# A gated mix of two attentions: path A's denominators inverted an iteration later, fetched by ScalarE, late products moved to the iteration's end

## The chip, the cores and the metric

The kernel runs on one core of a Trainium2 chip. The metric is the time of the whole launch on the device, in microseconds (us); before the change it is 987.2 us (median of three runs, 984.97 to 989.04).

## What is computed

```python
g = _sigmoid((x * gate_w).sum(-1, keepdims=True))
# path A, linear attention with a learned feature map, 16 heads of 28
phi_q = concat([softmax(pq), softmax(-pq)]); phi_k = the same of pk
kv  = einsum("bhsf,bhsd->bhfd", phi_k, v)
num = einsum("bhqf,bhfd->bhqd", phi_q, kv)
den = einsum("bhqf,bhf->bhq", phi_q, z) + 1e-6
a = (num / den) @ wo_A
# path B, softmax attention, 16 heads of 28
b = softmax(q k^T / sqrt(28)) v @ wo_B
out = g * a + (1 - g) * b          # 2048 tokens, 448 columns, float32
```

## The kernel before, in words

The order of the instructions on TensorE, VectorE, ScalarE and GpSimd is the order in which the code is written; only SyncE's transfers are ordered by a scheduler. Every transfer, on whatever queue, also takes the next of eight completion counters in turn, and waits until the transfer that had this counter before it has landed.

The change lies in one loop (L703), where path A's queries are handled and path B's values begin. Its iterations are counted here by q, from 0 to 26; y is q - 1. The 2048 queries are taken in eight blocks of 256, numbered 0 to 7. For one block b these steps follow each other:

- In iteration y = 2b + 4, `numer` (L522) forms the numerators of block b on TensorE in two PSUM banks `pn`. `normalize1` (L377) copies them with ScalarE into the SBUF tile `oUa` (L381); one row in 32 of it holds a denominator. Two small transfers spread these rows over 128 partitions, tile `dena` (L384). Before the change SyncE issues them.
- `normalize2` (L387): VectorE inverts `dena` (L389). Two transfers write the inverses to DRAM, `rda` (L393), and one transfer of 512 KB reads them back with each row repeated for 32 partitions, `rsa` (L394). Before the change it is called at y = 2b + 5, an odd iteration, behind the feature work.
- `normalize3` (L398): VectorE multiplies `oUa` by `rsa` (L400), at y = 2b + 8, in the middle of the iteration.
- `normalize4` (L403): ScalarE rounds the product to `oTa` (L408), and GpSimd forms what the rounding left (L409), at y = 2b + 9.
- `out_a` (L536) projects block b with `woA_s` on TensorE, 12 matmuls into `poa` for each 128 queries, at y = 2b + 10 and 2b + 11; ScalarE scales the result to `ga` (L544), which goes to DRAM (`gad`, L545).

Between these stand, in the same iterations: the projection of the queries `pq` (L109, 11 matmuls, to q = 15) with its features (`pcq`, `extq`, `featq`), the transposes of the features `pft` (L516) that ScalarE copies to `fT` (L519), the values of path B `pvb` (11 matmuls of L109, copied to `vb` by L691, from q = 18), and `mx_unit` (L238): four matmuls `pmd` and `pmb` (L260), two ScalarE operations `rl` (L264) and two VectorE operations on `pmb` and `rl` (L265, written "ISA" in the lists of order). From q = 19 to q = 25 an iteration holds two such units, one in its middle and one at its end.

PSUM is given out in turn: `pn`, `poa`, `pft`, `pq` and `pvb` share four banks in a ring, and the four banks of one `mx_unit` are used again by the next. So TensorE's next transposes wait for the ScalarE copy that empties the bank four places earlier in the ring.

Of the kernel before, what the change touches and what calls it, by code (L numbers as in the profile page):

```python
# [17 lines left out]
P = 128  # L18
# [3 lines left out]
DH = 28  # L22
GW = 112
NG = 4
NT = S // P
# [16 lines left out]
def gated_mix_kernel(ctx, tc, xT, wqkB, wvB, wvA, wkAT, wqAT, phi, woA, woB,  # L42
# [7 lines left out]
    nc = tc.nc  # L50
# [18 lines left out]
    def ps_mx(nm):  # L69
        return ps.tile([P, 512], F32, tag="mx", name=nm, bufs=psn[1])  # L70
# [94 lines left out]
    def take_acts():  # L165
        while acts:
            acts.pop(0)()
# [20 lines left out]
    def mx_query(gq):  # L188
        g, qb = divmod(gq, NQ)
        mxs[("qc", gq)] = mx_rows(mx_tile("qc", f"qc{gq}", 3), range(4), q_d[g], range(4), qb * 512)  # L190
# [19 lines left out]
    def pair_query(gq, hp):  # L210
        g, qb = divmod(gq, NQ)
        mxs[("qp", gq, hp)] = mx_rows(mx_tile("qc", f"qp{gq}_{hp}", 3), range(4), q_d[g],
                                      (2 * hp, 2 * hp + 1) * 2, qb * 512)

    def mx_fin():
        while mxs["fin"]:
            mxs["fin"].pop(0)()
# [20 lines left out]
    def mx_unit():  # L238

        u = mxs["u"]  # L240
        if u == NF:
            return
        mx_fin()
        mxs["u"] = u + 1
        gq, r = divmod(u, 16)
        g, qb = divmod(gq, NQ)
        c, qt = divmod(r, 4)
        hp, b = divmod(c, 2)
        col = 64 * gq + 16 * b + 4 * qt + 2 * hp
        if r in (4, 9) and gq + 1 < GM:  # L250
            pair_query(gq + 1, r // 9)
        if r == 4 and gq + 1 == GM:
            mx_query(GM)
        qc, kc = mxs[("qp", gq, hp)], mxs[("kp", g, c)]

        pm = [ps_mx(f"pm{'ddbb'[j]}{u}_{j % 2}") for j in range(4)]
        for j in range(4):
            i = (j + 2) % 4
            js = slice(32 * i, 32 * i + DH)
            nc.tensor.matmul(pm[j], qc[js, qt * P:(qt + 1) * P], kc[js, :], start=True, stop=True,  # L260
                             tile_position=(32 * i, 0))
        for i in range(2):
            rl = rlp.tile([P, 512], F32, tag="rl", name=f"rl{u}_{i}", bufs=psn[2])
            nc.scalar.activation(rl, pm[i], AF.Relu)  # L264
            nc.vector.tensor_tensor_reduce(rl, pm[2 + i], rl, 1.0, LOWEST, ALU.add, ALU.max,  # L265
                                           part[:, col + i:col + i + 1])
        if gq + 1 < GM and qt == 3 and qb == NQ - 1:
            pair_load(g + 1, c)
        if gq + 1 == GM and qt == 3:
            mx_load(GM // NQ, c)  # L270
        if r == 15:
            mx_reduce(gq)
# [104 lines left out]
    def normalize1(pool, pn, nm, n):  # L377

        oU = pool.tile([P, n, 512], F32, tag="oU", name=f"oU{nm}", bufs=2 * n - 1)
        for i in range(n):  # L380
            (nc.scalar.copy if n == 2 else nc.vector.tensor_copy)(oU[:, i, :], pn[i])  # L381
        den = pool.tile([P, n, 16], F32, tag="den", name=f"den{nm}", bufs=2)
        for i in range(n):
            nc.sync.dma_start(den[:, i, :], oU[DH:P:32, i, :])  # L384
        return oU, den

    def normalize2(pool, oU, den, nm, n):  # L387

        nc.vector.reciprocal(den, den)  # L389
        rd = dr.tile([4, n * 512], F32, tag=f"rd{n}", name=f"rd{nm}", bufs=2)  # L390
        rs = pool.tile([P, n, 512], F32, tag="rs", name=f"rs{nm}", bufs=n)
        for k in range(n):
            nc.sync.dma_start(rd[:, k * 512:(k + 1) * 512], den[:, k, :])  # L393
        nc.sync.dma_start(rs.rearrange("p n q -> p (n q)"),  # L394
                          rd.unsqueeze(1).to_broadcast([4, 32, n * 512]))
        return oU, rs

    def normalize3(oU, rs, n):  # L398

        (nc.gpsimd if n == 1 else nc.vector).tensor_mul(oU, oU, rs)  # L400
        return oU
# [58 lines left out]
    fk, va, fq, fT_of, num, oTs = {}, {}, {}, {}, {}, {}  # L460
# [242 lines left out]
    for i in range(2 * NT + 11):  # L703
        t, q = i, i - NT
        y = q - 1
        tb = y // 2
        take_acts()
        if t < NT and t % 2 == 0:
            mx_unit()
            passes = (55 if t < NT - 4 else 44) + (4 if t >= 4 else 0)  # L710
            pace["n"], pace["at"] = 4 if t >= 4 else 0, [k * passes // 4 for k in range(1, 4)]
        if q in (0, 1):
            take_exps()

        if t % 2 == 0 and 0 <= t - 4 < NT:
            kv_add(t - 4)
            kv_add(t - 3)
        if q == 2:
            bk_s.close()
            ta_s = ExitStack()  # L720
            ta = ta_s.enter_context(tc.tile_pool(name="ta", bufs=1, reuse_waits="tile"))
            stg = ta_s.enter_context(tc.tile_pool(name="stg", bufs=2, reuse_waits="tile"))
            KV = ta.tile([P, 2, P], F32, name="KV")
            kvT = kv_copy()
            ps_s_.close()
            ps = ps_s_.enter_context(tc.tile_pool(name="psq", bufs=1, space=PSUM, reuse_waits="tile"))
            psn[0] = 4
            woA_s = weights(3, "woA_s")
            wvB_s = weights(2, "wvB_s")
            take_exps()  # L730
        if t < NT:
            pk = ps_s(f"pk{t}")
            tok_major(pk, t, wkA_s, D, tick)
            fk[t] = features1(pk, f"k{t}", nc.gpsimd)
            take_exps(1)
        if 0 <= q < NT:
            pq = ps_s(f"pq{q}")
            tok_major(pq, q, wqA_s, D)
        if q == 0:
            fk[NT - 1] = features2(fk[NT - 1], f"k{NT - 1}")  # L740
        if q in (1, 2):
            fq[q - 1] = features2(fq[q - 1], f"q{q - 1}")
        if 0 <= q < NT:
            fq[q] = features1(pq, f"q{q}", nc.vector if q in (4, 6) else nc.gpsimd)
        if 0 <= t - 1 < NT - 1:
            fk[t - 1] = features2(fk[t - 1], f"k{t - 1}")
        if q in (0, 1) or q >= 8:
            mx_unit()
        if y >= 9 and y % 2 and tb - 4 < 8:
            oTs[tb - 4] = normalize4(ta, num.pop(tb - 4), f"a{tb - 4}", 2)  # L750
        if q > 0:
            take_exps(int(q < NT))
        if q == 3:
            kv_out(kvT)
        if 2 <= q - 1 < NT:
            fq[q - 1] = features2(fq[q - 1], f"q{q - 1}")
        take_subs()
        if t == 1:
            pair_load(0, 3)
        if y >= 8 and y % 2 == 0 and tb - 4 < 8:  # L760
            num[tb - 4] = normalize3(*num[tb - 4], 2)
        if y >= 5 and y % 2 and tb - 2 < 8:
            num[tb - 2] = normalize2(ta, *num[tb - 2], f"a{tb - 2}", 2)
        if t < NT:
            value_a(t)
            if t % 2 and t < NT - 4:
                proj_qk(NP + t // 2, ev)
        if q in (0, 1):
            proj_qk(NP + 6 + q, ev)
        take_lows()  # L770
        if 2 <= i < 6:
            fold(wqA_s, "q", i - 2)
        if q == 1:
            ev_s.close()
        if q == 2:
            part_loads("woA", woA, D, "woA")
            raws["wvB"] = [f32(ta.tile([P, 2, 512], F32R, tag="oT", name=f"wvB_raw{b}", bufs=4))[:, :, :D]
                           for b in (0, 2)]
            for i in range(2):
                nc.sync.dma_start(raws["wvB"][i], wvB[:, 2 * i:2 * i + 2, :])  # L780
        if q in (4, 6):
            split_part(woA_s, "woA", D, (q - 4) // 2, nc.gpsimd)
        if q in (8, 10):
            split_part(wvB_s, "wvB", D, (q - 8) // 2)
        if q == 1:
            gates()
        if y >= 4 and y % 2 == 0 and tb - 2 < 8:
            numer(tb - 2)
        if y < 9 or y % 2:
            if y >= 2 and y - 2 < NT:  # L790
                turn(y - 2)
        if 0 <= y - 10 < NT:
            out_a(y - 10)
            out_a2(y - 10)
        if y >= 9 and y % 2 == 0 and y - 2 < NT:
            turn(y - 2)
        if NT + 3 <= q < NT + 10:
            mx_unit()
        if q == NT + 6:
            ps_s_.close()  # L800
            ps = ps_s_.enter_context(tc.tile_pool(name="psv", bufs=1, space=PSUM, reuse_waits="tile"))
            psn[:2] = 2, 6
        if q == NT + 2:
            bd_s.close()
            vb = [value_tile(0)]
        if 0 <= q - NT - 2 < 8:
            value_b(q - NT - 2)
# [434 lines left out]
```

## Time and profile before

| what | value |
|---|---|
| time of the profiled execution | 986.38 us |
| span in its trace | 984.6 us |
| TensorE busy | 973.6 us, 99% |
| VectorE, ScalarE, GpSimd busy | 716.0, 752.2, 228.1 us |
| mean granted TensorE clock | 0.998 |
| moved by DMA | 84.49 MB, all on SyncE's queue but 1.44 MB of instructions |

The trace lists each instruction with its start, length, and what ended the idle time of its engine just before it. PE is TensorE, PEld its weight load, DVE VectorE, ACT ScalarE, POOL GpSimd, SPq the queue of SyncE. A matmul's length is modelled and overlaps the next; the distance between starts is the measure. The stage that the change touches lies between 204 and 332 us of the span.

### The profile page before, as it was taken

What the parts mean: (1) busy time and instruction counts of PE and PEld (TensorE: products, weight loads), DVE (VectorE), ACT (ScalarE), POOL (GpSimd) and SP (SyncE); (2) the same over time, 40 slices, a digit from 0 to 9 for tenths busy, and PEclk for the clock granted to TensorE, in tenths of its full rate; (3) what the DMA queues carried; (4) which work ended last, traced back from release to release, by engine and by line L of the source; (5) the groups of instructions that cost most, each with busy time, mean ns of one, the idle gap of its engine ahead of it and who ended that gap; (6) DMA issues with size and microseconds to landing.
All of it is one profiled execution on the core that took longest, in us unless ns stands there. A gap on an engine that the chain in (4) does not pass through costs nothing.

```text
span 984.6 us, 22550 instructions
## 1 busy us (share of the span) xinstructions
PE 973.6 (99%) x8510; PEld 602.9 (61%) x8510; DVE 716.0 (73%) x1338; ACT 752.2 (76%) x1442; POOL 228.1 (23%) x236
## 2 busy tenths in 40 slices
PE   9999999999999999999999999999999999999998
PEld 8777877787767765555555555545555555555555
DVE  5566767888735678888888888888888888885112
ACT  4455655577855688988988888888898898887662
POOL 1135435586732810031011011011011011010010
PEclk9999999999999999999999999999999999999999
DMA  8873110112223234121132121122231222100441
GB/s 295 315 255 114 37 53 32 44 51 73 96 91 100 85 120 130 38 62 41 62 93 69 39 63 41 60 82 66 69 83 41 64 63 65 41 21 30 142 150 57
DMA packets 56140, 84.49 MB, mean 86 GB/s; under 512 B 17216, under 2 KB 23984, under 8 KB 56032
## 3 DMA queue, kind: packets, MB, share of 16 engines
q1 hardware_dynamic: 56032, 83.06, 27.2%
q8 instruction: 67, 1.10, 0.5%
q14 instruction: 41, 0.34, 0.1%
HBM read 54.86 MB, written 27.78 MB: 84 GB/s over the span
## 4 chain that ended last, share of the span: by engine, by line
PE 89%; DMA 6%; DVE 2%; ACT 1%; issue 1%; SPq 0%; DVEq 0%; ACTq 0%
PE g L861 29%; PE pv L1006 26%; PE pk L127 4%; PE pva L127 4%; PE pqk L109 3%; PE g L288 3%; PE pq L109 3%; PE poa L109 3%; PE pob L109 3%; PE pmd L260 3%; DMA dena<-oUa 2%; PE pvb L127 2%; DMA qkd<-ev 2%; PE pvb L109 1%; DMA xraw<-in_xT_dram 1%
## 5 line engine op out<-in xcount | busy, mean ns | idle before, releaser
L869 ACT ACTIVATE p<-g 128x512 f32<-128x512 f32 x1020 | 525.6, 609 | 83.0 <-PE g L861 82.2
L295 DVE TENSOR_REDUCE part<-g 128x1 f32<-128x512 f32 x704 | 442.5, 684 | 83.9 <-PE g L288 82.4
L861 PEld LDWEIGHTS g<-qst,kst 32*128 32x128 f32 x3060 | 221.3, 183 | 215.2 <-DVE part L295 195.0
L861 PE MATMUL g<-qst,kst 32*128 32x512 f32 x3060 | 338.3, 420 | 0.1
L1006 PE MATMUL pv<-p,vb 128*32 128x512 f32 x2048 | 273.0, 605 | 0.0
L288 PE MATMUL g<-kc,qc 28*128 28x512 f32 x704 | 233.5, 495 | 0.0
L265 DVE CUSTOM_DVE_ANT_0 rl<-pmb,rl 128x512 f32<-128x512 f32 x160 | 103.2, 682 | 45.0 <-ACT rl L264 44.9
L400 POOL TENSOR_TENSOR oUb<-oUb,rsb 128x512 f32<-128x512 f32 x15 | 19.3, 1286 | 488.9 <-DMA rsb<-rdb 419.7
L264 ACT ACTIVATE rl<-pmd 128x512 f32<-128x512 f32 x160 | 87.6, 602 | 33.5 <-PE pmb L260 30.1
L288 PEld LDWEIGHTS g<-kc,qc 28*128 28x128 f32 x704 | 86.5, 182 | 0.3
L1006 PEld LDWEIGHTS pv<-p,vb 128*32 128x32 f32 x2048 | 40.6, 108 | 66.1 <-issue 64.2
L109 PE MATMUL pqk<-XH,wB 128*128 128x512 f32 x192 | 59.5, 398 | 0.8 <-DVE ev L569 0.8
L260 PE MATMUL pmb<-kp,qp 28*128 28x512 f32 x160 | 43.1, 498 | 3.3 <-DVE part L265 2.7
L109 PE MATMUL poa<-woA_s,oTa 128*128 128x448 f32 x192 | 45.1, 384 | 0.0
L568 ACT CAST ev<-pqk 128x512 fp32r<-128x512 f32 x28 | 16.0, 588 | 38.0 <-PE pqk L109 21.5
L1017 DVE SCALAR_TENSOR_TENSOR acc<-pob,gate,acc 128x448 f32<-128x448 f32 x12 | 8.2, 684 | 48.4 <-PE pob L109 48.4
L109 PEld LDWEIGHTS pqk<-XH,wB 128*128 128x128 f32 x192 | 35.3, 188 | 9.9 <-issue 1.5
L569 DVE TENSOR_TENSOR ev<-pqk,ev 128x512 fp32r<-128x512 f32 x28 | 18.9, 689 | 29.5 <-ACT ev L568 29.4
L260 PE MATMUL pmd<-kp,qp 28*128 28x512 f32 x160 | 40.1, 497 | 0.0
L109 PEld LDWEIGHTS poa<-woA_s,oTa 128*128 128x128 f32 x192 | 35.7, 193 | 7.0 <-issue 2.5
L127 PE MATMUL pk<-wkA_s,XH 128*128 128x448 f32 x128 | 39.4, 382 | 0.0
L109 PE MATMUL pq<-wqA_s,XH 128*128 128x448 f32 x128 | 37.4, 375 | 1.3 <-ACT oUa L381 1.3
(158 smaller groups left out, 1054.5 us busy)
## 6 DMA issues: line engine op xcount, KB each, us to landing
qkd<-ev SPq DMA_DIRECT2D x28, 512.0 KB
qst<-qkd SPq DMA_DIRECT2D x64, 112.0 KB
kst<-qkd SPq DMA_DIRECT2D x64, 112.0 KB
od<-oTb SPq DMA_DIRECT2D x48, 112.0 KB
rsa<-rda SPq DMA_DIRECT2D x8, 512.0 KB
oL<-od SPq DMA_DIRECT2D x8, 512.0 KB
rsb<-rdb SPq DMA_DIRECT2D x15, 256.0 KB
gad<-ga SPq DMA_DIRECT2D x16, 224.0 KB
```

The lines of the kernel that those rows point to most:

```text
L109: nc.tensor.matmul(dst, l, r, start=i == 0, stop=i == len(todo) - 1)
L127: nc.tensor.matmul(dst[:, :n], l, r, start=i == 0, stop=i == len(todo) - 1, skip_group_check=True)
L260: nc.tensor.matmul(pm[j], qc[js, qt * P:(qt + 1) * P], kc[js, :], start=True, stop=True, tile_position=(32 * i, 0))
L264: nc.scalar.activation(rl, pm[i], AF.Relu)
L265: nc.vector.tensor_tensor_reduce(rl, pm[2 + i], rl, 1.0, LOWEST, ALU.add, ALU.max, part[:, col + i:col + i + 1])
L288: nc.tensor.matmul(pm, mxs[("qc", gq)][js, qt * P:(qt + 1) * P], mxs[("kc", gq // NQ, kb)][js, :], start=True, stop=True, tile_position=(3 ...
L295: nc.vector.tensor_reduce(part[:, col:col + 1], pm, AX.X, ALU.max)
L400: (nc.gpsimd if n == 1 else nc.vector).tensor_mul(oU, oU, rs)
L569: nc.vector.tensor_sub(e[:, 1, :], pq, f32(e[:, 0, :]))
L861: nc.tensor.matmul(st[j], kst_of[(gq // NQ, kt // 4)][js, k, (kt % 4) * P:(kt % 4 + 1) * P], qst_of[gq][js, q, :], start=n == 0, stop=n == ...
L869: nc.scalar.activation(p, st[j], AF.Exp, scale=SCALE)
L1006: nc.tensor.matmul(pv[32 * j:32 * j + 32, :], vb[kt // 8][:, kt % 8, 4 * g + j, :], pt[j], start=kt == 0, stop=kt == NT - 1, tile_position ...
```

## The change

Three things are done, for path A alone (n = 2 in the code; path B calls the same functions with n = 1 and stays).

- The two transfers of a block's denominators are issued by ScalarE, behind its copies of the numerators, and no longer by SyncE.
- The inversion with its three transfers is done at y = 2b + 6, an even iteration, right behind the `mx_unit` in its middle, and no longer at y = 2b + 5.
- The products of blocks 4 to 7 (y = 16, 18, 20, 22) stand at the end of their iteration, behind its second `mx_unit` where there is one. Those of blocks 0 to 3 stay.

```diff
         for i in range(n):
-            nc.sync.dma_start(den[:, i, :], oU[DH:P:32, i, :])
+            (nc.scalar if n == 2 else nc.sync).dma_start(den[:, i, :], oU[DH:P:32, i, :])
         return oU, den
...
         if q in (0, 1) or q >= 8:
             mx_unit()
+        if y >= 6 and y % 2 == 0 and tb - 3 < 8:
+            num[tb - 3] = normalize2(ta, *num[tb - 3], f"a{tb - 3}", 2)
         if y >= 9 and y % 2 and tb - 4 < 8:
             oTs[tb - 4] = normalize4(ta, num.pop(tb - 4), f"a{tb - 4}", 2)
...
-        if y >= 8 and y % 2 == 0 and tb - 4 < 8:
+        if y >= 8 and y % 2 == 0 and y < NT and tb - 4 < 8:
             num[tb - 4] = normalize3(*num[tb - 4], 2)
-        if y >= 5 and y % 2 and tb - 2 < 8:
-            num[tb - 2] = normalize2(ta, *num[tb - 2], f"a{tb - 2}", 2)
...
         if NT + 3 <= q < NT + 10:
             mx_unit()
+        if y >= NT and y % 2 == 0 and tb - 4 < 8:
+            num[tb - 4] = normalize3(*num[tb - 4], 2)
```

The order of TensorE and of GpSimd stays as it was. On VectorE, in iterations q = 18 and 19, the inversion of block 6 (`dena_3333`) and the product of block 5 (`oUa_3202`) stand before the change like this:

```order
L389 RECIPROCAL dena_3333<-dena_3333 128x32
L265 ISA rl_0_3452,part<-pmb_0_3446,rl_0_3452 128x512
L265 ISA part 128x1
L265 ISA rl_1_3455,part<-pmb_1_3447,rl_1_3455 128x512
L265 ISA part 128x1
L400 TENSOR_TENSOR oUa_3202<-oUa_3202,rsa_3265 128x1024
L265 ISA rl_0_3507,part<-pmb_0_3501,rl_0_3507 128x512
L265 ISA part 128x1
L265 ISA rl_1_3510,part<-pmb_1_3502,rl_1_3510 128x512
L265 ISA part 128x1
```

After the change (some buffer numbers differ, the blocks are the same, block 6's denominators are `dena_3332`):

```order
L265 ISA rl_0_3446,part<-pmb_0_3440,rl_0_3446 128x512
L265 ISA part 128x1
L265 ISA rl_1_3449,part<-pmb_1_3441,rl_1_3449 128x512
L265 ISA part 128x1
L389 RECIPROCAL dena_3332<-dena_3332 128x32
L265 ISA rl_0_3506,part<-pmb_0_3500,rl_0_3506 128x512
L265 ISA part 128x1
L265 ISA rl_1_3509,part<-pmb_1_3501,rl_1_3509 128x512
L265 ISA part 128x1
L400 TENSOR_TENSOR oUa_3202<-oUa_3202,rsa_3307 128x1024
```

The inversion has moved behind the pair of operations of the `mx_unit` that it stood ahead of, and the product behind the second pair.

On ScalarE, in iteration q = 17, where block 6's numerators are copied, stands before the change:

```order
L381 COPY oUa_3330<-pn_0_3312 128x512
L381 COPY oUa_3330<-pn_1_3313 128x512
L544 ACTIVATE ga_3349<-poa_3336,gate 128x448
L519 COPY fT_3352<-pft_0_3353 128x3x128
L519 COPY fT_3352<-pft_3_3354 128x3x128
```

After it:

```order
L381 COPY oUa_3329<-pn_0_3311 128x512
L381 COPY oUa_3329<-pn_1_3312 128x512
L384 DMA dena_3332<-oUa_3329 128x1x16 x2
L544 ACTIVATE ga_3348<-poa_3335,gate 128x448
L519 COPY fT_3351<-pft_0_3352 128x3x128
```

Two transfers now stand in ScalarE's queue ahead of `ga` and `fT`. In the built program each waits for its own copy of ScalarE and for the transfer that last had its completion counter. For the second transfer of block 2 this is block 0's `rsa`, and for the second of block 6 it is block 4's `rsa`; the counters of the others were last raised by `dena` or `rda` transfers, or by short loads, of earlier iterations.

On SyncE, where block 4's inverses are written and read back (`rda_3110` before), the order was:

```order
L393 DMA rda_3110<-dena_3031 4x32x16 x2
L394 DMA rsa_3111<-rda_3110 128x1x1024
L384 DMA dena_3205<-oUa_3202 128x1x16 x2
L545 DMA gad_70<-ga_3221 128x448
L545 DMA gad_70<-ga_3294 128x448
```

After the change the same place reads:

```order
L393 DMA rda_3172<-dena_3031 4x32x16 x2
L545 DMA gad_70<-ga_3221 128x448
L394 DMA rsa_3173<-rda_3172 128x1x1024
L545 DMA gad_70<-ga_3288 128x448
```

The denominators have left the queue, and one `gad` now stands ahead of the broadcast `rsa`.

## The prediction

> **What bounds the kernel now.** I read the page's shares and the chain that ended last first, then the waits on the tile `dena`, then TensorE's own order of time where the chain leaves it.
>
> ```profile
> span 984.6 us, 22550 instructions
> PE 89%; DMA 6%; DVE 2%; ACT 1%; issue 1%; SPq 0%; DVEq 0%; ACTq 0%
> L384 SPq DMA_DIRECT2D dena<-oUa x16: 534/547/637, 206.7 to 287.4; - x16
> L389 DVE RECIPROCAL dena<-dena x8: 352/353/354, 214.0 to 295.1; 128x32 f32<-128x32 f32 x8
>   DMA dena<-oUa: 18.7, 6
> ```
>
> TensorE carries 89% of the chain. VectorE stands still 18.7 us in six of the eight inversions, until the denominators have landed. That is VectorE's idle time, not the kernel's: most of it lies beside full TensorE work. The two longest waits, and what TensorE does around them:
>
> ```profile
> 283.06 0.35 DVE L389 RECIPROCAL dena<-dena 128x32 f32<-128x32 f32 x1 [7.67 <-DMA dena<-oUa]
> 295.09 0.35 DVE L389 RECIPROCAL dena<-dena 128x32 f32<-128x32 f32 x1 [5.13 <-DMA dena<-oUa]
> ...
> 282.93 0.50 PE L260 MATMUL pmd<-kp,qp 28*128 28x512 f32 x2
> 284.03 1.10 PE L260 MATMUL pmb<-kp,qp 28*128 28x512 f32 x2 [0.59 <-DVE part L265]
> 285.06 0.67 PE L109 MATMUL pvb<-wvB_s,XH 128*128 128x448 f32 x2
> 296.06 1.11 PE L260 MATMUL pmb<-kp,qp 28*128 28x512 f32 x2 [2.14 <-DVE part L265]
> 297.09 4.05 PE L109 MATMUL poa<-woA_s,oTa 128*128 128x448 f32 x12
> 301.69 0.67 PE L109 MATMUL pvb<-wvB_s,XH 128*128 128x448 f32 x2
> 308.06 0.67 PE L109 MATMUL pvb<-wvB_s,XH 128*128 128x448 f32 x2 [0.34 <-ACT ga L544]
> 313.55 0.49 PE L260 MATMUL pmd<-kp,qp 28*128 28x512 f32 x2
> 313.99 0.67 PE L109 MATMUL pvb<-wvB_s,XH 128*128 128x448 f32 x2
> ```
>
> The reader is to see a ruler in the starts of `pvb`. An undisturbed iteration takes 313.99 - 308.06 = 5.93 us, and from the second `pmd` to `pvb` 313.99 - 313.55 = 0.44 us. In the disturbed stretch:
>
> - 285.06 - 282.93 = 2.13 us instead of 0.44: 1.69 us lost. `pmb` waits for banks that VectorE has not read, because VectorE waits for block 6's denominators.
> - From the `pvb` at 285.06 to that at 301.69 lie two iterations, 16.63 us and not 2 x 5.93 = 11.86: 4.77 us lost, by block 7's denominators.
> - 308.06 - 301.69 = 6.37 instead of 5.93: 0.44 us lost in the aftermath.
>
> Together 6.9 us. The other waits of the 18.7 us fall where TensorE has queued work. A part of the 4.77 us is no wait but slow matmuls: the 12 `poa` from 297.09 last 4.05 us, and the granted clock (the column of 1.00, 1.00, 0.63, 0.94) drops behind the hole:
>
> ```profile
> 219.00:224.00 5.00, 4.61 (x55) 3.17 (x53) 4.93 (x14) 5.00 (x9) 4.80 (x6) 1.00 0.25 94
> 293.00:297.00 4.00, 1.74 (x7) 0.67 (x5) 1.79 (x6) 1.43 (x3) 1.85 (x2) 1.00 0.19 51
> 297.00:301.00 4.00, 4.00 (x13) 3.13 (x12) 2.17 (x5) 0.30 (x1) 0.00 (x0) 0.63 0.45 127
> 301.00:305.00 4.00, 4.00 (x22) 2.88 (x22) 1.31 (x4) 2.39 (x5) 0.00 (x0) 0.94 0.38 135
> ```
>
> **Why the denominators are late.** Block 4's broadcast is the clean case:
>
> ```profile
> 259.33 1.16 SPq L393 DMA_DIRECT2D rda<-dena  x2
> 261.94 0.54 SPq L394 DMA_DIRECT2D rsa<-rda  x1
> 262.58 1.13 SPq L384 DMA_DIRECT2D dena<-oUa  x2
> 270.70 0.35 DVE L389 RECIPROCAL dena<-dena 128x32 f32<-128x32 f32 x1 [1.60 <-DMA dena<-oUa]
> ```
>
> The inverses take 261.94 - 259.33 = 2.6 us from their issue until `rsa` can be issued. `dena`, issued 0.6 us behind `rsa`, lands only at 270.7, 8.1 us later. It crawls behind the 512 KB of `rsa`, which moves at 94 GB/s with a DMA share of 0.25 (the window from 219). I take 8.0 us from the issue of `rsa` to its landing.
>
> **The change, part by part.** *The inversion, an iteration later.* A block's `dena` is issued in iteration y = 2b + 4 and needed in y = 2b + 6, behind the `mx_unit`: in the last blocks that is two iterations, some 11 us, against 8.1 us of landing. So all 18.7 us of waits go, and TensorE gets back its 6.9 us. What is late next is `rsa`: inversion plus 0.4 us to the issue, 2.6 and 8.0 us make 11 us, and the product of blocks 4 to 7 now stands two iterations and a bit (over 12 us) behind the inversion. That fits; the product's own 1.2 us, behind the second `mx_unit`, delays nobody until the next unit. Count and length of inversions, products and transfers stay.
>
> *The transfers on ScalarE.* The trace shows none there. On SyncE one takes 0.55 us, so a block's two cost ScalarE between nothing and 1.2 us. I take 0.55: the first can be issued while the second copy runs, the second can't. Eight blocks make 4.4 us of ScalarE's time. In most blocks ScalarE idles behind the copies anyway, as it does here:
>
> ```profile
> 223.72 1.13 ACT L381 COPY oUa<-pn 128x512 f32<-128x512 f32 x2
> 224.66 1.17 ACT L519 COPY fT<-pft 128x512 f32<-128x512 f32 x2
> 226.94 0.53 ACT L421 COPY pcq<-pq 128x448 f32<-128x448 f32 x1 [1.11 <-PE pq L109]
> 231.05 1.09 ACT L519 COPY fT<-pft 128x512 f32<-128x512 f32 x2
> 231.81 1.09 PE L529 MATMUL pn<-fT,KV 57*32 57x256 f32 x32
> 269.75 1.14 ACT L381 COPY oUa<-pn 128x512 f32<-128x512 f32 x2
> 271.89 0.64 ACT L544 ACTIVATE ga<-poa,gate 128x448 f32<-128x448 f32 x1 [0.99 <-PE poa L109]
> ```
>
> That idle time, near 1 us, hides 0.55 us. Were the cover gone, each block would cost TensorE up to 1.2 us.
>
> *The two added waits.* Two of the sixteen transfers wait for a broadcast, and ScalarE's whole queue waits with them.
>
> ```profile
> 214.79 0.60 DVE L424 TENSOR_REDUCE extq<-pcq 128x16 f32<-128x448 f32 x1
> 261.18 0.68 DVE L265 CUSTOM_DVE_ANT_0 rl<-pmb,rl 128x512 f32<-128x512 f32 x1
> 273.09 1.09 PE L516 MATMUL pft<-ident,featq 128*128 128x128 f32 x8
> 273.94 2.69 PE L109 MATMUL poa<-woA_s,oTa 128*128 128x448 f32 x12
> ```
>
> Block 2's second transfer waits for block 0's `rsa`. That inversion now follows `extq`, which ends at 215.4, or 215.1 without the old inversion ahead of it; plus 0.4, 2.6 and 8.0 it lands at 226.1. ScalarE is there at 224.85, so it is held 1.25 us and issues for 0.55. Of these 1.8 us, 1.1 us was idle before `pcq`, some 0.7 to 0.9 us stays and is carried through a full queue to the `fT` copies at 231.05. `pn` at 231.81 needs them: 0.8 us on TensorE.
>
> Block 6's second transfer waits for block 4's `rsa`. The inversion now follows the operation that ends at 261.86; its `rsa` is issued at 264.9 and lands at 272.9. ScalarE arrives at 270.9, is free at 273.4, and `ga` starts 1.5 us later than at 271.89. The transposes at 273.09 need the bank that `ga` empties, and `poa` at 273.94 the bank of an `fT` copy behind it: 1.3 us on TensorE. Below this lies nothing (the broadcast lands in time); above it 2.3 us, if `rsa` needs 9.
>
> For lags in the other six blocks I take 0.2 us. Sum: -6.9 + 0.8 + 1.3 + 0.2 = -4.6 us. The profiled execution took 986.4 us (2 us more than its span), so 981.8 us; it lies 0.8 us under the median of 987.2, and the three runs spread over 4 us.
>
> [...]
>
> **The rivals.**
>
> 1. *The waits cost nothing.* The broadcasts land before ScalarE is there, because they no longer share the queue with `dena`. Then the whole 6.9 us stay: 979.5 us. For it: each transfer is small and the estimate of 8.0 us comes from a landing behind two transfers. Against: 8.1 us for `dena` leaves little below 7.5.
> 2. *No change to speak of.* ScalarE pays 0.55 us in every block on the path (4.4 us), and the two waits 2.1: 6.5 us against 6.9, so 986 us. For it: ScalarE is busy all 5.00 us from 219 to 224. Against: idle times of 0.4 to 1.5 us behind the other copies.
> 3. *Slower: ScalarE's queue becomes the bound of the stage.* A queue held for both transfers, 1.2 us in each of eight blocks, makes 9.6 us, and the waits of blocks 2 and 6 at the upper landing 1.8 + 2.3 = 4.1 us more: 13.7 - 6.9 = +6.8, so 993 us. It decides if the hold exceeds the idle time behind the copies, near 1 us; at 0.55 it doesn't. [...]
> 4. *The waits only move.* If `dena` took over 11 us, the inversion would wait as before, at another place, and the 6.9 us would stay lost: 986 us and more. Nothing in the rows reaches 11.
>
> **How the numbers follow.** Forecast 0.50, rival 1 0.17, rivals 2 and 4 0.20, rival 3 0.13. The predicted time is 981.8 us. The range, 978 to 989, takes in the forecast with the bounds of its waits, rivals 1 and 2, and the spread of the runs; it leaves out most of rival 3. A measurement can tell about 0.5%, 4.9 us, from no change. The forecast lies 5.4 us under the median, barely outside: faster gets rival 1 and two thirds of the forecast, 0.50; same gets 0.36; slower 0.14.
>
> **What would show it.** Right: no inversion waits for `dena`, `pvb` starts 5.9 us apart from its second on, no clock below 1.00 near 300, two gaps on ScalarE behind the copies of blocks 2 and 6 that end when a broadcast lands, and TensorE waiting for `ga` behind the second. Wrong: ScalarE's lengths or gaps growing by over 1 us in every block; inversions or products that wait; `mx_unit` waiting on VectorE because the product now stands ahead of the next unit.

## The result, and the profile after

The changed kernel takes 983.7 us (median of 20 runs, 980.25 to 987.07), the kernel before 986.33 us (20 runs beside it, 984.47 to 989.25). The ratio is 0.9971, with a 95% interval of 0.9958 to 0.9984: about 2.9 us less, between 1.6 and 4.1. That is a real gain, but inside the 0.5% that was called no change. The profiled execution took 981.96 us, its span is 980.2 us; before it was 986.38 and 984.6.

I read the page's span and chain first, then the rows of the two lines on which the change rests. The page of the changed kernel:

```profile
span 980.2 us, 22541 instructions
PE 94%; ACT 2%; DMA 2%; DVE 1%; issue 1%; ACTq 0%; SPq 0%; POOL 0%; DVEq 0%; POOLq 0%
```

TensorE's share of the chain has risen from 89 to 94%, that of DMA has fallen from 6 to 2%, and ScalarE's has risen from 1 to 2%. The inversion (L389) and the denominators' transfers (L384), each by its line (durations are least, median, most, in ns):

```profile
L389 DVE RECIPROCAL dena<-dena x8: 340/348/351, 214.8 to 296.3; 128x32 f32<-128x32 f32 x8
its engine sat idle before it (us, times) until:
...
L384 ACTq DMA_DIRECT2D dena<-oUa x16: 529/537/1105, 206.4 to 283.9; - x16
```

Nothing stands below "sat idle": the 18.7 us of VectorE's waits are gone. A transfer costs ScalarE's queue 0.54 us. TensorE in order of time, by the same ruler as before:

```profile
204.35 1.09 PE L529 MATMUL pn<-fT,KV 57*32 57x256 f32 x32
...
233.34 1.15 PE L529 MATMUL pn<-fT,KV 57*32 57x256 f32 x32 [1.25 <-ACT fT L519]
...
269.06 1.09 PE L529 MATMUL pn<-fT,KV 57*32 57x256 f32 x32
275.21 1.10 PE L516 MATMUL pft<-ident,featq 128*128 128x128 f32 x8 [1.10 <-ACT ga L544]
276.14 2.71 PE L109 MATMUL poa<-woA_s,oTa 128*128 128x448 f32 x12
281.45 1.09 PE L529 MATMUL pn<-fT,KV 57*32 57x256 f32 x32
285.11 0.50 PE L260 MATMUL pmd<-kp,qp 28*128 28x512 f32 x2
285.55 0.67 PE L109 MATMUL pvb<-wvB_s,XH 128*128 128x448 f32 x2
291.49 0.67 PE L109 MATMUL pvb<-wvB_s,XH 128*128 128x448 f32 x2
297.43 0.67 PE L109 MATMUL pvb<-wvB_s,XH 128*128 128x448 f32 x2
303.78 0.67 PE L109 MATMUL pvb<-wvB_s,XH 128*128 128x448 f32 x2 [0.34 <-ACT ga L544]
```

The rows of before that were not shown yet:

```profile
204.67 1.10 PE L529 MATMUL pn<-fT,KV 57*32 57x256 f32 x32
...
268.12 1.09 PE L529 MATMUL pn<-fT,KV 57*32 57x256 f32 x32
...
279.27 1.09 PE L529 MATMUL pn<-fT,KV 57*32 57x256 f32 x32
```

From `pmd` at 285.11 to `pvb` it is 0.44 us again, and from `pvb` to `pvb` 5.94 us, twice. Up to there two places have become longer: from the first `pn` to that of block 6, 64.71 us where it was 63.45 (+1.26), and from that to the next `pn` 12.39 where it was 11.15 (+1.24). The sum of the stretch, from the `pn` near 204 to the `pvb` that stood at 308.06: 1.26 + 1.24 - 1.69 - 4.75 - 0.02 = -3.96 us, and 0.3 us came in ahead of it (204.35 where it was 204.67).

Both long places have one cause. SyncE's broadcast of block 0, then ScalarE and VectorE of the changed kernel at blocks 2 and 6, and last TensorE's transposes behind block 2's copies:

```profile
218.04 0.55 SPq L394 DMA_DIRECT2D rsa<-rda  x1
224.08 3.48 ACTq L384 DMA_DIRECT2D dena<-oUa  x2
227.04 1.23 DVE L400 TENSOR_TENSOR oUa<-oUa,rsa 128x1024 f32<-128x1024 f32 x1 [1.17 <-DMA qp<-qkd]
227.60 1.07 ACT L519 COPY fT<-pft 128x512 f32<-128x512 f32 x2 [3.06 <-PE pmd L260]
...
271.43 2.90 ACTq L384 DMA_DIRECT2D dena<-oUa  x2
273.74 1.22 DVE L400 TENSOR_TENSOR oUa<-oUa,rsa 128x1024 f32<-128x1024 f32 x1 [1.70 <-DMA rsa<-rda]
274.43 0.63 ACT L544 ACTIVATE ga<-poa,gate 128x448 f32<-128x448 f32 x1 [2.55 <-DMA qp<-qkd]
...
228.25 0.66 PE L516 MATMUL pft<-ident,featq 128*128 128x128 f32 x4 [0.62 <-ACT fT L519]
```

Two transfers take 1.1 to 1.2 us where nothing holds them, as in e4 below; here they take 3.48 and 2.90 us, since the second is held. It leaves when VectorE's product of the block two earlier starts (227.04, 273.74), that is, when that block's broadcast lands, for block 0 9.0 us after its issue. The releasers named for `fT` and `ga` (`pmd`, `qp`) are only what came last by the profile; `pmd` cannot hold a copy that stands behind a held queue. At block 2 TensorE waits twice: 0.62 us with the transposes at 228.25, for the first `fT` copies behind the held transfer, and 1.25 us with `pn` at 233.34.

What no single profile shows is the spread. Six of the 20 runs had a mean granted clock of 1.000 and took 980.25 to 981.96 us; six had 0.996 or 0.997 and took 985.01 to 987.07. The profiled execution is one of the first six.

### The profile page after: what moved, and what is told of

Read it like the earlier page. It is cut to its first block, busy times and chain, and to the rows that moved or that the text cites. A ratio compares the mean times of both kernels' runs of the same rounds, so it can differ in the third digit from the quotient of the medians.

```text
span 980.2 us, 22541 instructions
## 1 busy us (share of the span) xinstructions
PE 970.2 (99%) x8510; PEld 601.8 (61%) x8510; DVE 716.5 (73%) x1338; ACT 751.6 (77%) x1442; POOL 227.6 (23%) x236
## 4 chain that ended last, share of the span: by engine, by line
PE 94%; ACT 2%; DMA 2%; DVE 1%; issue 1%; ACTq 0%; SPq 0%; POOL 0%; DVEq 0%; POOLq 0%
PE g L863 29%; PE pv L1008 27%; PE pqk L109 6%; PE pk L127 4%; PE pva L127 4%; PE poa L109 4%; PE g L288 4%; PE pmd L260 3%; PE pob L109 3%; PE pq L109 2%; PE pvb L127 2%; PE pvb L109 2%; PE pqk L630 1%; DMA rsa<-rda 1%; PE pft L516 1%
```

## The experiments

My theory after the result: moving the inversion closes the holes (6.4 us), and ScalarE's two waits for an old broadcast give 2.5 us back. The rivals: it is the issue by ScalarE that helps; every issue costs ScalarE; the late products matter. A second theory, on the spread, came with the profile of e6: the holes sometimes drop TensorE's clock. Each comparison is against the kernel before on the same chip.

| run | what is done | median us | ratio to before, 95% interval |
|---|---|---|---|
| changed kernel | all three parts | 983.7 | 0.9971, 0.9958 to 0.9984 |
| e1 | issue by ScalarE alone | 979.81 | 0.9934, 0.9921 to 0.9947 |
| e2 | order alone, SyncE issues | 979.66 | 0.9930, 0.9918 to 0.9942 |
| e3 | changed, products back | 984.74 | 0.9978, 0.9965 to 0.9991 |
| e4 | changed, broadcast in four | 979.35 | 0.9924, 0.9912 to 0.9936 |
| e5 | changed, SyncE in blocks 2 and 6 | 980.05 | 0.9941, 0.9926 to 0.9957 |
| e6 | changed, ScalarE in 2 and 6 only | 984.74 | 0.9980, 0.9966 to 0.9995 |
| e7 | before, broadcast in four | 979.51 | 0.9936, 0.9920 to 0.9952 |
| e8 | inversion moved alone | 980.83 | 0.9946, 0.9931 to 0.9960 |
| e11 | e2 with the broadcast in four | 979.32 | 0.9930, 0.9917 to 0.9944 |

### e1 and e2: one part of the change alone

e1 is the kernel before with this edit; e2 is the changed kernel with this edit undone.

```diff
-            nc.sync.dma_start(den[:, i, :], oU[DH:P:32, i, :])
+            (nc.scalar if n == 2 else nc.sync).dma_start(den[:, i, :], oU[DH:P:32, i, :])
```

> Before, with one part of the change alone: ScalarE issues the denominators; inversions and products stay where they were. My theory says that the 6.4 us of holes come from a denominator transfer that SyncE issues behind a 512 KB broadcast. Issued by ScalarE it has the lead: block 6's leaves near 271 us and is wanted at 275.4, block 7's near 281.7 and is wanted at 290, against about 3 us of landing. So both holes close without the move: -6.4 us, plus 0.5 to 1 us where ScalarE waits for an older broadcast (block 2, perhaps 4 and 7): about -5.5 us, a ratio near 0.9945. Rival (the later inversion is what brings the gain): the inversions still wait for the denominators and the time stays within 1 us of before.

> The changed kernel, but SyncE issues the denominators as before. Theory (the later inversion brings the gain, ScalarE's two waits for a broadcast cost 2.5 us of it): both holes close and nothing holds ScalarE, so about -6.4 us against before (ratio near 0.9935), 2 to 2.5 us below the changed kernel. Rival 1 (the issue by ScalarE is what brings the gain): no better than before. Rival 2 (SyncE's queue, held by the denominators, sends the broadcasts late): products wait for rsa on VectorE for 1 us or more in several blocks, and the gain is 4 us or less.

Both hold, and the rival that only one of them helps falls: either part alone gives 6.5 to 6.9 us, together they give 2.9. e2 lies 4.0 us below the changed kernel's median, more than the 2 to 2.5 that I gave the holds: what e9 below shows beside them is a lower clock and longer holds. In e1 the inversions of blocks 6 and 7 stand where they stood before and find their denominators there (block 5's still waits 1.36 us); ScalarE's holds have become short. VectorE and ScalarE of e1:

```profile
223.66 2.48 ACTq L384 DMA_DIRECT2D dena<-oUa  x2
226.19 1.08 ACT L519 COPY fT<-pft 128x512 f32<-128x512 f32 x2 [2.07 <-DMA rsa<-rda]
...
274.83 0.35 DVE L389 RECIPROCAL dena<-dena 128x32 f32<-128x32 f32 x1
280.64 2.41 ACTq L384 DMA_DIRECT2D dena<-oUa  x2
287.75 0.35 DVE L389 RECIPROCAL dena<-dena 128x32 f32<-128x32 f32 x1
```

Here the releaser of `fT` is named as it should be: the broadcast `rsa`. With the inversion an iteration earlier, it lands earlier, and ScalarE is held about 1.3 us at block 2, not 2.3. The second hold of 1.3 us stands at another place: in e1's program block 6's transfers wait for no broadcast, and block 7's second one waits for block 5's. At block 2, then, the price is a product of both parts: the issue by ScalarE brings the wait, the later inversion makes it long.

### e3 and e8: the products back in the middle

e3 is the changed kernel, e8 is e2, each with the third part undone:

```diff
-        if y >= 8 and y % 2 == 0 and y < NT and tb - 4 < 8:
+        if y >= 8 and y % 2 == 0 and tb - 4 < 8:
             num[tb - 4] = normalize3(*num[tb - 4], 2)
...
-        if y >= NT and y % 2 == 0 and tb - 4 < 8:
-            num[tb - 4] = normalize3(*num[tb - 4], 2)
```

> The changed kernel with the products of all blocks in the middle of the iteration, as before; inversion and issue by ScalarE as changed. Theory (the late products are worth nothing here: VectorE stands behind its inversion anyway until the broadcast of block 4 lands, and has 1.2 us to spare elsewhere): within 0.5 us of the changed kernel. Rival (a product ahead of the next unit's reads holds TensorE): 1.2 us in each of up to three iterations, up to 3.6 us slower than the changed kernel.

> The inversion moved and nothing else: SyncE issues, the products of all blocks stay in the middle. The earlier run with the products back had ScalarE's waits in it and could not tell an effect below 1 us. Theory: the product of block 5 stands right behind an inversion and waits some 1 us for its broadcast, which VectorE has to spare: within 0.5 us of the kernel with the order changed and SyncE's issue (ratio 0.993). Rival: the products hold the next unit's reads, 1 to 3 us slower than that (ratio 0.994 to 0.996).

e3's times can't tell: its interval lies over that of the changed kernel, and its runs spread from 981.19 to 987.38. Its profile can. From its `pvb` near 285 to the fourth it is 18.23 us:

```profile
284.82 0.66 PE L109 MATMUL pvb<-wvB_s,XH 128*128 128x448 f32 x2
...
303.05 0.67 PE L109 MATMUL pvb<-wvB_s,XH 128*128 128x448 f32 x2 [0.34 <-ACT ga L544]
```

In the changed kernel it is 303.78 - 285.55 = 18.23 us too. So beside the issue by ScalarE the late products are worth nothing in this stretch, as I expected. e8 goes against me. Its median is 1.2 us above e2's; the two intervals overlap, but the profile shows the same 1.2 us. VectorE and TensorE of e8:

```profile
284.00 1.23 DVE L400 TENSOR_TENSOR oUa<-oUa,rsa 128x1024 f32<-128x1024 f32 x1 [2.29 <-DMA rsa<-rda]
285.90 1.10 PE L260 MATMUL pmb<-kp,qp 28*128 28x512 f32 x2
...
296.56 1.23 DVE L400 TENSOR_TENSOR oUa<-oUa,rsa 128x1024 f32<-128x1024 f32 x1 [1.39 <-DMA rsa<-rda]
298.46 1.11 PE L260 MATMUL pmb<-kp,qp 28*128 28x512 f32 x2
...
283.44 0.67 PE L109 MATMUL pvb<-wvB_s,XH 128*128 128x448 f32 x2
302.98 0.66 PE L109 MATMUL pvb<-wvB_s,XH 128*128 128x448 f32 x2 [0.34 <-ACT ga L544]
```

The product stands right behind the inversion and waits 2.29 and 1.39 us for its broadcast; the `mx_unit` behind it then waits for VectorE (its `pmb` take 1.1 us, where the others take 0.50). From the `pvb` near 283 to the fourth it is 19.54 us in e8 and 18.34 in e2. So the late products are worth about 1.2 us where SyncE issues the denominators. In e3 the inversion of block 6 starts at 282.74 and in e8 at 281.36, but the product behind it starts at nearly the same time (283.84 and 284.00), when its broadcast lands: what comes 1.4 us later behind ScalarE's holds waits that much less for it (0.76 us in e3).

### e4 and e7: the broadcast cut in four

Both cut the broadcast into four transfers, from one source row to 32 partitions each; e4 does it to the changed kernel, e7 to the kernel before.

```diff
-        nc.sync.dma_start(rs.rearrange("p n q -> p (n q)"),
-                          rd.unsqueeze(1).to_broadcast([4, 32, n * 512]))
+        if n == 1:
+            nc.sync.dma_start(rs.rearrange("p n q -> p (n q)"),
+                              rd.unsqueeze(1).to_broadcast([4, 32, n * 512]))
+        else:
+            for j in range(4):
+                nc.sync.dma_start(rs[32 * j:32 * j + 32].rearrange("p n q -> p (n q)"),
+                                  rd[j:j + 1].to_broadcast([32, n * 512]))
```

> The changed kernel with each 512 KB broadcast cut into four transfers of 128 KB, one source row to 32 partitions each. In the changed kernel the broadcast moves at 94 GB/s with a DMA share of 0.24, a quarter of the engines, and block 0's lands 8.9 us after its issue. Theory (few engines make it late, and its lateness makes ScalarE wait): with all engines it lands some 4 us after its issue (3 us of fixed time as rda's, and 1.4 us of moving), the waits behind the copies of blocks 2 and 6 vanish, and 2 to 2.5 us come back: near -6 us against before. Rival (the lateness is not a matter of engines): it lands 8 us after its issue as before, and with more transfers on the eight completion counters ScalarE waits in more blocks (two in 2, 4, 5, 6 or 7): slower than the changed kernel by 1 us or more.

> Before, with nothing but each broadcast cut into four transfers of one source row to 32 partitions. Theory (the holes of before come from denominators queued behind a broadcast that moves on a quarter of the engines): the denominators land some 4 us instead of 8 us after the broadcast's issue; block 6's 1.69 us close, of block 7's 4.75 us some 1.5 are left, for its denominators now leave 1.7 us later: about -5 us, between -4 and -6.5. Rival (the small transfer is late for another reason, its own latency on a busy ring): the denominators land as late as before and leave 1.2 to 1.7 us later: no gain, 1 to 2 us slower than before.

e4 gives back all that the waits took: 979.35 us, 4.4 below the changed kernel's median, and its five runs lie within 1.2 us. ScalarE of e4 at blocks 2 and 6:

```profile
224.32 1.16 ACTq L384 DMA_DIRECT2D dena<-oUa  x2
...
270.07 1.16 ACTq L384 DMA_DIRECT2D dena<-oUa  x2
```

In its built program the second transfers of blocks 2, 4, 5 and 6 and both of block 7 wait for a broadcast, more than in the changed kernel. None is held (a block's two take 1.16 to 1.18 us), for the broadcasts have landed. One window of the changed kernel and one of e4, each while a broadcast moves (the last two columns are the DMA share and GB/s):

```profile
225.00:226.00 1.00, 1.00 (x6) 0.93 (x6) 0.80 (x3) 0.00 (x0) 0.00 (x0) 1.00 0.24 94
```

```profile
267.00:268.00 1.00, 1.00 (x22) 0.37 (x20) 0.88 (x1) 1.00 (x4) 1.00 (x2) 1.00 0.76 246
```

The view takes its share over 16 engines, so 0.24 is the work of 3.8 of them. That the broadcast runs on four is my estimate from this share; no view shows the engines one by one. Cut in four, it moves in the window of e4 at a share of 0.76 and 246 GB/s, where the changed kernel shows 0.24 and 94.

e7 is the surprise: this one edit alone, with nothing of the change, gives 979.51 us. SyncE and VectorE of e7 at block 6 and 7:

```profile
274.79 0.56 SPq L384 DMA_DIRECT2D dena<-oUa  x1
277.86 0.35 DVE L389 RECIPROCAL dena<-dena 128x32 f32<-128x32 f32 x1 [1.86 <-DMA dena<-oUa]
288.83 0.35 DVE L389 RECIPROCAL dena<-dena 128x32 f32<-128x32 f32 x1
```

Issued behind a split broadcast, block 6's denominators land 3.1 us after their issue (274.79 to 277.86), and not 8 us. Block 7's are there in time, and from 283.97 on TensorE's `pvb` start 5.97, 5.97 and 6.39 us apart, without a hole. I had expected 5 us with a rest of block 7's hole, but block 6's inversion comes 5 us earlier (277.86, before 283.06), and with it all that stands behind it on SyncE, block 7's denominators too.

### e5 and e6: the two blocks apart

```diff
-            (nc.scalar if n == 2 else nc.sync).dma_start(den[:, i, :], oU[DH:P:32, i, :])
+            (nc.scalar if n == 2 and nm not in ("a2", "a6") else nc.sync).dma_start(den[:, i, :], oU[DH:P:32, i, :])
```

e6 has `nc.scalar if nm in ("a2", "a6")` in that place.

> The changed kernel, but SyncE issues the denominators of blocks 2 and 6; ScalarE issues those of the other six. In the built program no transfer of ScalarE waits for a broadcast any more. Theory (the two waits are the whole cost of the issue by ScalarE): as where SyncE issues all of them, ratio near 0.993, about -6.5 us. Rival (ScalarE pays for every issue, some 0.5 us in each block): only a quarter of the 3.9 us between the changed kernel and the one with SyncE comes back: about -3.9 us.

> The counterpart: ScalarE issues the denominators of blocks 2 and 6 alone, SyncE the other six. In the built program the second transfers of these two blocks wait for the broadcasts of blocks 0 and 4, as in the changed kernel. Theory: as the changed kernel, ratio near 0.997, with waits of 1 to 2 us behind the copies of these two blocks and the same wide spread of the runs. Rival (every issue costs): three quarters of the loss are gone, about -5.7 us.

Six of the eight blocks on ScalarE cost next to nothing (980.05 us); two, 2 and 6, cost all of it (984.74 us). The rival by which every issue costs is out, also by e4 against e11: 979.35 with all transfers on ScalarE, 979.32 with all on SyncE. In e6 ScalarE is held at these two blocks as in the changed kernel (two transfers take 2.97 and 3.57 us). TensorE waits less at block 2 than it does there (0.96 us, the row below; at block 6 it is 1.73), but behind both holes the clock falls:

```profile
233.06 1.17 PE L529 MATMUL pn<-fT,KV 57*32 57x256 f32 x32 [0.96 <-ACT fT L519]
```

Two windows of e6, right behind the holes (the column ahead of the DMA share is the granted clock, 0.63 and 0.68):

```profile
233.00:237.00 4.00, 3.94 (x40) 2.91 (x41) 3.97 (x10) 3.71 (x8) 3.81 (x4) 0.63 0.17 61
...
277.00:281.00 4.00, 3.92 (x17) 3.52 (x18) 1.31 (x4) 4.00 (x10) 1.48 (x2) 0.68 0.31 107
```

### e9 and e10: the changed kernel's profile again

Nothing is edited.

> The changed kernel once more, for its profile. Of its 20 runs six had a mean granted clock of 1.000 and took 980.25 to 981.96 us, the profiled one among them; 14 had 0.996 to 0.999 and took 982.42 to 987.07. Theory (the holes that ScalarE's waits open sometimes drop TensorE's clock): with a clock below 1.000 the profile shows it at 0.5 to 0.7 in a window right behind the hole of block 2 (near 233 us), of block 6 (near 275) or both, and nowhere else between 200 and 340 us, and each drop costs 1.3 to 2 us. Rival (the spread comes from elsewhere, the start or the later stages): the clock drops outside that stretch, and TensorE's starts inside it are those of the profile at hand.

> The same kernel a second time, since three in ten runs show no drop. The same two expectations.

e10 took 981.74 us at a clock of 1.000: as the first profile. e9 took 986.46 us at 0.997, and its drops stand right behind the two holes; between 200 and 340 us the clock is 1.00 outside these 4 us windows and their neighbours. Two windows, then TensorE and ScalarE of e9:

```profile
233.00:237.00 4.00, 3.14 (x38) 2.21 (x39) 3.93 (x8) 4.00 (x9) 3.81 (x5) 0.75 0.18 70
...
280.00:284.00 4.00, 4.00 (x14) 3.55 (x14) 0.67 (x4) 2.50 (x6) 3.32 (x4) 0.65 0.33 122
```

```profile
223.82 4.26 ACTq L384 DMA_DIRECT2D dena<-oUa  x2
228.12 1.07 ACT L519 COPY fT<-pft 128x512 f32<-128x512 f32 x2 [3.84 <-DMA rsa<-rda]
233.86 1.15 PE L529 MATMUL pn<-fT,KV 57*32 57x256 f32 x32 [1.25 <-ACT fT L519]
...
248.85 1.09 PE L529 MATMUL pn<-fT,KV 57*32 57x256 f32 x32
...
277.95 1.09 PE L516 MATMUL pft<-ident,featq 128*128 128x128 f32 x8 [1.77 <-ACT ga L544]
278.88 4.27 PE L109 MATMUL poa<-woA_s,oTa 128*128 128x448 f32 x12
```

The 12 `poa` behind block 6's hole take 4.27 us, in the first profile 2.71. That is one drop: 1.56 us. From the `pn` at 233.86 to the next it is 14.99 us, where the first profile has 246.78 - 233.34 = 13.44: 1.55 us, the other. The rest of e9's 4.5 us more span is in longer holds (4.26 where it was 3.48 at block 2; TensorE waits 1.77 where it was 1.10 at block 6: 0.8 and 0.7 us). The row of `fT` at 228.12 names block 0's broadcast as what ends the hold of block 2; why that lands later in e9 than in the first profile, where `fT` starts at 227.60, no view shows. The first profile, by contrast, in these two windows:

```profile
233.00:237.00 4.00, 3.66 (x45) 2.72 (x46) 3.92 (x11) 3.99 (x8) 3.81 (x4) 1.00 0.14 55
...
280.00:284.00 4.00, 4.00 (x49) 2.77 (x48) 1.58 (x5) 2.59 (x5) 1.00 (x3) 1.00 0.38 131
```

Over all runs the low clock goes with the holds. The changed kernel, e3 and e6 hold ScalarE at blocks 2 and 6: 34 of their 44 runs have a mean clock of 0.998 or less. e2, e4, e5, e7, e8 and e11 don't: 3 of their 33 runs have. Where those three lose it, no profile shows.

### e11: a version with no wait at all

It is e2 with the broadcast cut as in e4.

> The inversion moved, products late, SyncE issues the denominators, and each broadcast cut in four: the version without any wait that the runs so far have shown. Theory (all 6.4 us of holes and some 0.3 us of short waits are gone in each of the single cures, and nothing else is to be had from these transfers): ratio near 0.9925, not below the kernel with the split alone by more than 0.5 us. Rival (the cures add up): 1 us or more below it, ratio 0.991.

979.32 us: the cures don't add up. With the holes closed, nothing is left for these transfers to give. e1, e2, e4, e7 and e11 can't be told apart; all are faster than both kernels. e1 does it with one line, e7 without moving any work, and e4 and e11 have the narrowest spread.

## Why the prediction was right, and where it was not

The range held the time, and the mechanism was right on both sides of the sum. The time moved by less than the 0.5% that was called no change, though, an outcome that had a chance of 0.36 where "faster" had 0.50. By its steps, against the profiled execution:

- **All waits for the denominators go, and the holes with them.** Right. Expected 1.69 and 4.77 us, measured 1.69 and 4.75.
- **The aftermath, 0.44 us.** Wrong: 303.78 - 297.43 = 6.35 us, and it was 6.37. It is no aftermath: `ga` stands behind the casts of `oTa` in that iteration, so `pvb` waits 0.34 us in the changed kernel as before, and in the profile of every experiment.
- **Block 2's wait, 0.8 us.** Undersized: the interval up to block 6 has grown by 1.26 us, net of short inversion waits that went (in e4, which has no hold, the same interval is 63.11 us, 0.34 less than before). The hold itself thus costs 1.6 us, twice what was taken. The broadcast took 227.0 - 218.0 = 9.0 us from its issue to its landing, and 8.0 was taken; and TensorE waits not only for the second `fT` copies, as the sum had it, but also for the first (0.62 us).
- **Block 6's wait, 1.3 us.** Right: 1.24.
- **Other blocks, 0.2 us; a transfer's price on ScalarE, 0.55 us hidden.** The price is right: 0.54 us each, and no cost that e4 against e11 shows.
- **The late products fit.** Right for TensorE: nothing waits for them. But the two iterations and a bit don't hold for block 4, whose iteration has no second `mx_unit`: its product stands 11.05 us behind its inversion (262.69 to 273.74) and waits 1.70 us for its broadcast. Back in the middle the products cost 1.2 us where SyncE issues (e8), and nothing in the changed kernel (e3).

The profiled pair moved by 4.4 us, 4.6 was forecast. That it is so close is partly luck. The profiled execution is one of the six at a clock of 1.000; and 0.44 us of aftermath did not come back and block 2 cost more than was taken, while 0.3 us came in ahead of the stretch, from nothing in the sum. All runs together moved by 2.9 us (by the ratio), and the step that failed lies there: the sum let the slow matmuls (12 `poa` in 4.05 us where 2.69 is usual, 1.4 us) go with the hole of before, and gave the new holes no clock price. In the profiled execution that is so; in 14 of 20 runs the clock is below 1.000. In e9, such a run, the two drops cost 1.55 us each, and longer holds another 1.5; how the 1.7 us between the profiled execution and the median divide between the two, no run shows. The slow matmuls of before stand behind a wait of 2.14 us; the drops of e6 and e9 came behind waits of 0.96 to 1.77 us.

Of the rivals, none came in the changed kernel. The first (waits that cost nothing, 979.5 us) is what e4 makes of it; the second and third fall with e5 against e6, which show that an issue as such costs nothing; the fourth with the inversion's rows.

What stays open is when a hole drops the clock. At block 2 the length doesn't decide: `pn` waited 1.25 us in the first profile, with full clock behind it, 1.25 us in e9, with 0.75, and 0.96 us in e6, with 0.63. (e9 also waited longer ahead of it, 1.36 us for the transposes where it was 0.62; e6 didn't wait there.) At block 6 the drops stand behind 1.73 and 1.77 us, and full clock behind 1.10 us in the first profile and 1.21 in e10. What decides it from run to run, no run here shows.

## What to carry to other kernels

The transfers that ScalarE's own queue issued made ScalarE wait here for what they waited for, also for an old transfer that only shared a completion counter (the two transfers took 3.48 us at block 2 and 2.90 at block 6, where e4 shows 1.16): look in the built program at what that is, and put the issue where nobody waits behind it. When a small transfer is late, look at the one ahead of it: here cutting a broadcast that moved at a DMA share of 0.24 gave 6.3 us by itself (e7). Moving the work around it gave 6.5 us or more in either of two ways, and 2.9 in both at once. And price a hole in TensorE twice, once for its length and once for the clock behind it (1.55 us for each drop in e9), over several runs and not in the one that was profiled.

## What the runs showed of the hardware

- Behind waits of 0.96 to 1.77 us in TensorE's work the granted clock was 0.63 to 0.75 in a window of 4 us (e6, e9), at a cost of 1.55 us for each drop in e9; behind waits of 1.10 and 1.25 us in the first profile it was 1.00. Of the 20 runs of the changed kernel, the six at 1.000 span 1.7 us; all 20 span 6.8 us.
- In the changed kernel's profile the broadcast of 512 KB landed 9.0 us after its issue in block 0 and 7.95 us in block 4 (265.79 to 273.74); it moved at 94 GB/s. Cut into four, each from one source row to 32 partitions, the DMA share rose from 0.24 to 0.76 in e4, and a small transfer behind it landed in 3.1 us in e7.
- One transfer of 8 KB took 0.54 us of ScalarE's queue (median of 16 in the changed kernel), and all 16 together cost nothing that e4 against e11 shows (979.35 and 979.32 us).
